# GpSimd issues most loads of a decode kernel, one packet per DMA engine and load

## The chip, the cores and the metric

The kernel runs on one core of a Trainium2 chip. A core has five engines, each with its own instruction stream: TensorE (PE: matrix products), VectorE (DVE), ScalarE (ACT), GpSimd (POOL) and SyncE (SP, which only issues transfers and waits). Sixteen DMA engines carry data from HBM into the core's on-chip memory; a transfer is issued by an instruction on one of the engines' streams, and ends by raising a semaphore by 16, one for each DMA engine. Other engines wait for semaphores to reach a value.

The metric is the device time of one execution in microseconds (us), as the median of the runs.

## What is computed

One new token attends to a cache, and a gated MLP of the same token is mixed in:

```python
g = sigmoid((x * gate_w).sum(-1, keepdims=True))          # one number
q = (x @ wq)                                              # 512 -> 32 heads x 128
scores = einsum("bhqd,bhkd->bhqk", q, k_cache) * Dh**-0.5 # 32 heads, 65536 cached rows
p = softmax(scores);  o = einsum("bhqk,bhkd->bhqd", p, v_cache)
a = o.reshape(1, 1, 4096) @ wo
b = (silu(x @ w_gate) * (x @ w_up)) @ w_down              # 512 -> 1792 -> 512
out = g * a + (1 - g) * b
```

All data are bf16. K and V have 32 heads x 65536 rows x 128, so 16.8 MB per head and cache and 1074 MB in all; wq and wo have 4.2 MB each, the three MLP weights 1.8 MB each. Each cached number is used once.

## The kernel before

One on-chip buffer, `ring`, holds four "places" of 8.39 MB, 64 KB per partition: K_A and K_B for the first and second half of a head's keys, V_A and V_B for its values. The places of a pair overlap: K_B begins at the middle of K_A, and V_B a quarter into V_A, so a load into one may start when the shared rows of the other have been used. `kv_dram[kind][h, u]` is half `u` of head `h`, laid out so that each of 128 partitions takes 256 consecutive rows, 64 KB in one piece. Weights use bytes that are free at the time (WQ among the V places at the start; WO, WG, WU and WD among the K places at the end).

For each head VectorE turns K in 32 pieces of 16 rows per partition (`turn`, L314, a blockwise transpose into four small buffers `kt`; semaphore `ktd` counts the pieces). TensorE multiplies each piece by the query (`scores`, L401, into the PSUM bank `psS`). When all 32 are done, VectorE takes the maximum per partition (L338, `s_mx`), GpSimd the maximum over partitions (L216, `s_ar`), ScalarE the exponentials with their sums (L251, `s_exp`), GpSimd the total of the sums (L218, `s_L`), and VectorE turns the probabilities (L340, `s_pb`). Then TensorE multiplies V: the rows of V_A in two parts (`flow`, L417; `va1` after rows 64 to 255), and, after the first half of the next head's scores, those of V_B (`vbd` when finished).

The order of the loads is written out by hand on SP's stream (L143 to L197), each load behind the wait that says its place is free. Per head `r` there are four: `K_A` of the next head when the first half of `K_B` has been turned (`ktd`), V_B when `va1` says that the rows of V_A it covers are done, `K_B` of the next head when the upper half of the new `K_A` has been turned (`ktd`), and V_A of the next head when V_B is done (`vbd`). `head(r, late)` holds this order; a loop runs it 30 times and once more with the two loads of `wo` added. At the start the q weights are issued first (L136), then K's first places in halves: upper half of K_A, its lower half (`s_k0a`), upper half of K_B (`s_k0b`), lower half of K_B. VectorE begins with the upper half of K_A (`A_ORDER`). At the end the last V_B place is cut into parts (`PARTS`, with the semaphores `MARKS`), and w_down into four, so that little work is left after the last landing. ScalarE issues only the two small inputs and the result.

GpSimd clears a few tiles, makes four copies of pieces of an identity matrix, and then does the two reductions over partitions per head, each behind its wait (L214 to L218).

Of the kernel before, what the change touches and what calls it, by code (L numbers as in the profile page):

```python
# [6 lines left out]
KB = 1024  # L7
CH = 16
NB = 4
K_A, K_B = 0, 32 * KB  # L10
V_A, V_B = 96 * KB, 112 * KB
# [6 lines left out]
ET = mybir.EngineType  # L18
# [8 lines left out]
def bass_gated_mix__mha_block_cached__swiglu_ffn__decode_kernel(  # L27
# [11 lines left out]
    out: bass.AP,  # L39
):  # L40
    _, H, S, Dh = A_k_cache.shape
    D = A_wq.shape[0]
    F = B_w_gate.shape[1]
    Dc = D // P
    FC = F // P
    ROWS = S // (2 * P)
    NCH = ROWS // CH
    SCALE = float(Dh) ** -0.5
    assert Dh == 128 and D == 512 and F % P == 0 and ROWS == 256 and H == 32
    L = H - 1  # L50
    A_ORDER = list(range(NCH // 2, NCH)) + list(range(NCH // 2))
    B_ORDER = list(range(NCH))
    PER = 2 * NCH

    with ExitStack() as ctx:
# [6 lines left out]
        def sem(name):  # L62
            return ctx.enter_context(nc.semaphore(name))
# [47 lines left out]
        sm = {n: sem(n) for n in names.split()}  # L111
# [4 lines left out]
        kv_dram = {"k": A_k_cache[0].rearrange("h (u p r) d -> h u p (r d)", u=2, p=P),  # L116
                   "v": A_v_cache[0].rearrange("h (u p r) d -> h u p (r d)", u=2, p=P)}

        def at(byte, n):
            return ring[:, byte // 2:byte // 2 + n]  # L120

        WQ, WO, WG, WU, WD = 144 * KB, 0, 0, 14 * KB, 64 * KB
        PARTS = ((192, 256), (0, 64), (64, 128), (128, 168), (168, 184), (184, 192))
        FLOW = 3
        MARKS = ("s_vb", "s_p2", "s_p3", "s_p4", "s_p5", "s_p6")
        WD_CUT = FC - 3
# [15 lines left out]
        @block.sync  # L142
        def _(sp):  # L143
            def load(dst, src, s):
                sp.dma_start(dst, src).then_inc(sm[s], 16)  # L145

            def place(kind, h, u, s):
                byte = {"k": (K_A, K_B), "v": (V_A, V_B)}[kind][u]
                src = kv_dram[kind][:, u]
                if isinstance(h, int):  # L150
                    src = src[h]
                else:
                    src = src[bass.ds(h, 1)].rearrange("h p n -> (h p) n")
                load(at(byte, ROWS * Dh), src, s)

            k0 = kv_dram["k"][0, 0]
            k1 = kv_dram["k"][0, 1]
            half = ROWS * Dh // 2
            load(at(K_A + 2 * half, half), k0[:, half:2 * half], "s_ka")
            load(at(K_A, half), k0[:, 0:half], "s_k0a")  # L160
            load(at(K_B + 2 * half, half), k1[:, half:2 * half], "s_k0b")
            sp.wait_ge(sm["ktd"], NCH // 2)
            load(at(K_B, half), k1[:, 0:half], "s_kb")
            sp.wait_ge(sm["s_q"], 1)
            place("v", 0, 0, "s_va")

            def head(r, late):
                sp.wait_ge(sm["ktd"], r * PER + (PER - NCH // 2))
                place("k", r + 1, 0, "s_ka")
                sp.wait_ge(sm["va1"], r + 1)  # L170
                place("v", r, 1, "s_vb")
                if late:
                    wo_dram = A_wo.rearrange("(p j) n -> p (j n)", j=32)
                    for q in range(2):
                        sp.wait_ge(sm["ktd"], r * PER + (PER + 3 * NCH // 4 + q * NCH // 4))
                        load(at(WO + q * 16 * KB, 16 * D), wo_dram[:, q * 16 * D:(q + 1) * 16 * D], "s_wo")
                sp.wait_ge(sm["ktd"], r * PER + (PER + NCH // 2))
                place("k", r + 1, 1, "s_kb")
                sp.wait_ge(sm["vbd"], r + 2)
                place("v", r + 1, 0, "s_va")  # L180

            with nc.Fori(0, L - 1, engines=[ET.SP]) as i:
                head(i, False)
            head(L - 1, True)
            sp.wait_ge(sm["s_wod"], 1)
            load(at(WG, Dc * F), B_w_gate.rearrange("(p c) f -> p (c f)", c=Dc), "s_wg")
            load(at(WU, Dc * F), B_w_up.rearrange("(p c) f -> p (c f)", c=Dc), "s_wu")
            sp.wait_ge(sm["ktd"], PER * H)
            wd_dram = B_w_down.rearrange("(p c) n -> p (c n)", c=FC)
            load(at(WD, WD_CUT * D), wd_dram[:, 0:WD_CUT * D], "s_wd")  # L190
            last = kv_dram["v"][L, 1]
            for n, ((r0, r1), s) in enumerate(zip(PARTS, MARKS)):
                if n == 1:
                    sp.wait_ge(sm["va1"], H)
                load(at(V_B + r0 * 256, (r1 - r0) * Dh), last[:, r0 * Dh:r1 * Dh], s)
            for j, s in ((FC - 3, "s_wd1"), (FC - 2, "s_wd2"), (FC - 1, "s_wd3")):
                load(at(WD + 2 * j * D, D), wd_dram[:, j * D:(j + 1) * D], s)  # L197

        @block.gpsimd
        def _(pool):  # L200
            nc.gpsimd.memset(xTz[:], 0.0).then_inc(sm["s_qd"], 1)
            nc.gpsimd.memset(qd[:], 0.0).then_inc(sm["s_qd"], 1)
            for m, n in enumerate(MARKS[1:]):
                nc.gpsimd.memset(hbuf[:, m], 0.0).then_inc(sm[n], 16 * L)
            nc.gpsimd.memset(hot[:], 0.0).then_inc(sm["s_hot"], 1)
            pool.wait_ge(sm["s_id"], 1)
            pool.wait_ge(sm["s_hot"], 1)
            nc.gpsimd.tensor_copy(hot[:, 31:128:32], ident[:, P - 4:P])
            for je in range(4):
                off = 64 * (je // 2) + je % 2  # L210
                last = nc.gpsimd.tensor_copy(sel[:, je, :].rearrange("p (g d) -> p g d", g=4),
                                             ident[:, off:off + 63:2].unsqueeze(1).to_broadcast([P, 4, 32]))
            last.then_inc(sm["s_sel"], 1)
            for h in range(H):  # L214
                pool.wait_ge(sm["s_mx"], h + 1)
                nc.gpsimd.partition_all_reduce(amx, mxs, P, RMAX).then_inc(sm["s_ar"], 1)  # L216
                pool.wait_ge(sm["s_exp"], h + 2)
                nc.gpsimd.partition_all_reduce(Lt, rsum, P, RADD).then_inc(sm["s_L"], 1)  # L218

        @block.scalar  # L220
        def _(act):
# [342 lines left out]
```

## Time and profile before

| | before |
|---|---|
| median of 3 runs | 2513.63 us (2513.57 to 2513.91) |
| span of the profiled execution | 2512.5 us; the page gives no other time of it |
| read from HBM | 1087.64 MB, 433 GB/s over the span |
| busy: PE, DVE, ACT, POOL | 1510.1, 1249.7, 43.0, 25.9 us |
| large loads (144 packets each) | 144, all issued by SP |

The span runs from the program's first instruction to the end of its last; a run's time holds also what lies around it. PE's busy time is modelled and overlaps itself, so 60% says nothing about how near TensorE is to its best. A DMA's row has its issuing instruction's time only; how long the data took is told by the time from issue to landing, which includes the time it stood behind earlier loads. The slices divide the span into 40 pieces of 62.8 us; a digit 9 means nine tenths or more.

### The profile page before, as it was taken

What the parts mean: (1) busy time and instruction counts of PE and PEld (TensorE: products, weight loads), DVE (VectorE), ACT (ScalarE), POOL (GpSimd) and SP (SyncE); (2) the same over time, 40 slices, a digit from 0 to 9 for tenths busy, and PEclk for the clock granted to TensorE, in tenths of its full rate; (3) what the DMA queues carried; (4) which work ended last, traced back from release to release, by engine and by line L of the source; (5) the groups of instructions that cost most, each with busy time, mean ns of one, the idle gap of its engine ahead of it and who ended that gap; (6) DMA issues with size and microseconds to landing.
All of it is one profiled execution on the core that took longest, in us unless ns stands there. A gap on an engine that the chain in (4) does not pass through costs nothing.

```text
span 2512.5 us, 25250 instructions
## 1 busy us (share of the span) xinstructions
PE 1510.1 (60%) x10158; PEld 574.4 (23%) x10158; DVE 1249.7 (50%) x1213; ACT 43.0 (2%) x142; POOL 25.9 (1%) x81
## 2 busy tenths in 40 slices
PE   5565655755656556566465565565655655656568
PEld 1222221222222222222222221222221222222222
DVE  5464553644545536446455364464553644645534
ACT  0000000000000000000000000000000000000000
POOL 0000000000000000000000000000000000000000
PEclk9877877878778777778787787777877777778779
DMA  9999999999999999999999999999999999999999
GB/s 418 434 434 434 434 434 434 434 434 434 434 434 434 434 434 434 434 434 434 434 434 434 434 434 434 436 435 435 435 435 435 434 434 435 434 436 434 434 433 395
DMA packets 20749, 1087.73 MB, mean 433 GB/s; under 512 B 2308, under 2 KB 2695, under 8 KB 2951
## 3 DMA queue, kind: packets, MB, share of 16 engines
q1 hardware_dynamic: 20736, 1087.64, 100.0%
q8 instruction: 4, 0.07, 0.0%
q14 instruction: 3, 0.02, 0.0%
q10 hardware_dynamic: 6, 0.00, 0.0%
HBM read 1087.64 MB, written 0.00 MB: 433 GB/s over the span
## 4 chain that ended last, share of the span: by engine, by line
DMA 75%; DVE 15%; issue 7%; PE 2%; DVEq 0%; SPq 0%; ACT 0%; POOL 0%
DMA ring<-in_A_k_cache_dram 74%; DVE kt L314 15%; PE psS L401 2%; DMA ring<-in_A_v_cache_dram 1%; DVEq L311 0%; SPq L145 0%; PE psW L417 0%; DVE st L325 0%; PE psY L423 0%; ACT pa L251 0%; DVE pb L340 0%; DVE st L338 0%; DVEq L324 0%; DVE fin L359 0%; SPq L136 0%
## 5 line engine op out<-in xcount | busy, mean ns | idle before, releaser
L401 PE MATMUL psS<-kt,zq 128*128 128x512 bf16 x4096 | 1132.7, 426 | 851.7 <-DVE kt L314 833.2
L314 DVE STREAM_TRANSPOSE kt<-ring 128x1024 uint32<-128x1024 uint32 x1024 | 1163.1, 1206 | 936.4 <-DMA ring<-in_A_k_cache_dram 936.4
L401 PEld LDWEIGHTS psS<-kt,zq 128*128 128x128 bf16 x4096 | 386.8, 104 | 1583.9 <-DVE kt L314 1120.7
L417 PE MATMUL psW<-ring,pb 128*4 128x512 bf16 x3584 | 253.5, 444 | 103.5 <-DVE pb L340 102.4
L417 PEld LDWEIGHTS psW<-ring,pb 128*4 128x4 bf16 x3584 | 93.9, 97 | 261.3 <-issue 184.4
L327 DVE COPY brow<-psW 128x512 f32<-128x512 f32 x32 | 22.1, 691 | 120.3 <-PE psW L417 120.3
L408 PEld LDWEIGHTS psO<-pb,ring 128*128 128x128 bf16 x2048 | 56.8, 98 | 0.6 <-DMA ring<-in_A_v_cache_dram 0.6
L408 PE MATMUL psO<-pb,ring 128*128 128x1 bf16 x2048 | 56.5, 163 | 0.4 <-DMA ring<-in_A_v_cache_dram 0.2
L330 DVE TENSOR_SCALAR lt<-psO,st,sc 128x4 f32 x32 | 9.4, 294 | 89.1 <-PE psO L408 89.1
L452 PE MATMUL psO<-id,brow 128*128 128x1 f32 x256 | 33.7, 253 | 25.6 <-DVE brow L327 24.8
L340 DVE STREAM_TRANSPOSE pb<-pa 128x512 bf16<-128x512 bf16 x32 | 22.8, 711 | 48.7 <-ACT pa L251 48.7
L249 ACT ACTIVATE st<-st 128x1 f32<-128x1 f32 x32 | 6.5, 203 | 2353.9 <-POOL st L216 2353.9
L338 DVE TENSOR_REDUCE st<-psS 128x1 f32<-128x512 f32 x32 | 22.1, 692 | 37.4 <-PE psS L401 37.4
L452 PEld LDWEIGHTS psO<-id,brow 128*128 128x128 f32 x256 | 31.0, 191 | 41.7 <-DVE brow L327 40.4
L216 POOL PARTITION_ALL_REDUCE st<-st x32 | 11.2, 351 | 2416.5 <-DVE st L338 2416.5
L251 ACT ACTIVATE pa<-psS,st 128x512 bf16<-128x512 f32 x32 | 22.0, 687 | 1.0
L428 PE MATMUL psF<-ring,om 128*1 (+1 forms) x32 | 13.1, 410 | 2.7 <-DMA ring<-in_A_wo_dram 2.7
L512 PE MATMUL psY<-ring,hot 128*128 (+1 forms) x32 | 13.6, 424 | 0.0
L218 POOL PARTITION_ALL_REDUCE st<-st x32 | 12.3, 384 | 36.4 <-ACT pa L251 36.4
L256 ACT COPY zq<-qd 128x16 bf16 x31 | 7.7, 248 | 0.0
L251 ACT ACTIVATION_READ_ACCUMULATOR pa<-psS,st 128x1 f32 x32 | 6.2, 193 | 0.0
L428 PE MATMUL psF<-ring,kt 128*1 128x512 bf16 x11 | 4.0, 542 | 2.9 <-DVE kt L353 2.9
(87 smaller groups left out, 53.2 us busy)
## 6 DMA issues: line engine op xcount, KB each, us to landing
ring<-in_A_k_cache_dram SPq DMA_DIRECT2D x4, 4096.0 KB, 27.5
ring<-in_A_v_cache_dram SPq DMA_DIRECT2D x3, 2048.0 KB, 17.3
ring<-in_A_wq_dram SPq DMA_DIRECT2D x1, 4096.0 KB, 12.3
ring<-in_A_wo_dram SPq DMA_DIRECT2D x2, 2048.0 KB, 10.5
ring<-in_B_w_gate_dram SPq DMA_DIRECT2D x1, 1792.0 KB, 20.6
ring<-in_B_w_up_dram SPq DMA_DIRECT2D x1, 1792.0 KB, 24.4
ring<-in_B_w_down_dram SPq DMA_DIRECT2D x1, 1408.0 KB, 12.8
ring<-in_A_v_cache_dram SPq DMA_DIRECT2D x1, 1280.0 KB, 20.8
```

Source lines behind the costliest of these rows:

```text
L218: nc.gpsimd.partition_all_reduce(Lt, rsum, P, RADD).then_inc(sm["s_L"], 1)
L251: nc.scalar.activation(pa[:], psS[:], ACT.Exp, bias=nbias, scale=SCALE, accum_out=rsum).then_inc(sm["s_exp"], 1)
L314: nc.vector.transpose(o, src).then_inc(sm["ktd"], 1)
L327: nc.vector.tensor_copy(brow[:], psW[:]).then_inc(sm["s_flc"], 1)
L338: nc.vector.reduce_max(mxs, psS[:], AX_X).then_inc(sm["s_mx"], 1)
L340: nc.vector.transpose(pb[:], pa[:]).then_inc(sm["s_pb"], 1)
L401: last = nc.tensor.matmul(psS[:], zw[je][c], ktb[n % NB][:, je // 2, :, je % 2], start=first and je == 0, stop=stop and je == 3)
L408: last = nc.tensor.matmul(psO[:, 0:1], at(base + r * 256, Dh), pb[:, col:col + 1], start=first and n == 0, stop=stop and n == len(rows) - 1)
L417: last = nc.tensor.matmul(psW[g:g + 4, :], pb[:, col:col + 97:32], at(base + r * 256, 4 * Dh), start=first and n < 4, stop=stop and n >= l ...
L428: return nc.tensor.matmul(psF[0:1, :], lhs, rhs, start=first, stop=stop)
L452: nc.tensor.matmul(psO[:, 0:1], brow[:, e * Dh:(e + 1) * Dh], id4[:, e:e + 1], start=e == 0, stop=False)
L512: return nc.tensor.matmul(psY[:], hot[:, bass.ds(31 - j, P)], w, start=first, stop=stop)
```

## The change

SP keeps eleven loads: the q weights, the lower half of the first K_A, the upper half of the first K_B, the last five parts of the last V place and the last three rows of `w_down`. The other 133 move to GpSimd's stream and are issued there with `single_packet=True`, which asks that what one DMA engine carries of one load be one packet. Waits and sizes of the loads are the same, except for two: the first half of K_A now waits for the q weights to have landed (`s_wq`), and the first part of the last V place stands behind the wait for the last maximum (`s_mx`). GpSimd's two reductions per head (`top`, `total`) stand among the loads; what was a loop on SP is written out for all heads on GpSimd.

```diff
         @block.sync
         def _(sp):
             def load(dst, src, s):
                 sp.dma_start(dst, src).then_inc(sm[s], 16)
...
             half = ROWS * Dh // 2
-            load(at(K_A + 2 * half, half), k0[:, half:2 * half], "s_ka")
-            load(at(K_A, half), k0[:, 0:half], "s_k0a")
-            load(at(K_B + 2 * half, half), k1[:, half:2 * half], "s_k0b")
-            sp.wait_ge(sm["ktd"], NCH // 2)
-            load(at(K_B, half), k1[:, 0:half], "s_kb")
-            sp.wait_ge(sm["s_q"], 1)
-            place("v", 0, 0, "s_va")
-
-            def head(r, late):
...
+            load(at(K_A, half), kv_dram["k"][0, 0, :, 0:half], "s_k0a")
+            load(at(K_B + 2 * half, half), kv_dram["k"][0, 1, :, half:2 * half], "s_k0b")
+            last = kv_dram["v"][L, 1]
+            sp.wait_ge(sm["va1"], H)
+            for (r0, r1), s in zip(PARTS[1:], MARKS[1:]):
+                load(at(V_B + r0 * 256, (r1 - r0) * Dh), last[:, r0 * Dh:r1 * Dh], s)
...
         @block.gpsimd
         def _(pool):
...
+            def load(dst, src, s):
+                nc.gpsimd.dma_start(dst, src, single_packet=True).then_inc(sm[s], 16)
...
-            for h in range(H):
+            pool.wait_ge(sm["s_wq"], 16)
+            load(at(K_A + 2 * half, half), kv_dram["k"][0, 0, :, half:2 * half], "s_ka")
+            pool.wait_ge(sm["ktd"], NCH // 2)
+            load(at(K_B, half), kv_dram["k"][0, 1, :, 0:half], "s_kb")
+            pool.wait_ge(sm["s_q"], 1)
+            place("v", 0, 0, "s_va")
+
+            def top(h):
                 pool.wait_ge(sm["s_mx"], h + 1)
                 nc.gpsimd.partition_all_reduce(amx, mxs, P, RMAX).then_inc(sm["s_ar"], 1)
+
+            def total(h):
                 pool.wait_ge(sm["s_exp"], h + 2)
                 nc.gpsimd.partition_all_reduce(Lt, rsum, P, RADD).then_inc(sm["s_L"], 1)
...
```

Three places matter. On GpSimd, the start and the first head: before, the setup of the reductions (an ISA row without a tile) and the first two heads' reductions follow each other directly.

```order
L211 COPY sel<-ident 128x128 x4
L216 ISA
L216 ISA st<-st 128x1 [waits s_mx]
L218 ISA st<-st 128x1 [waits s_exp]
L216 ISA st<-st 128x1 [waits s_mx]
L218 ISA st<-st 128x1 [waits s_exp]
```

After, on the same engine, from the same copies to the end of the first head and the K place that opens the second:

```order
L179 COPY sel<-ident 128x128 x4
L167 DMA ring<-in_A_k_cache_dram 128x16384 [waits s_wq]
L167 DMA ring<-in_A_k_cache_dram 128x16384 [waits ktd]
L167 DMA ring<-in_A_v_cache_dram 128x32768 [waits s_q]
L167 DMA ring<-in_A_k_cache_dram 128x32768 [waits ktd]
L191 ISA
L191 ISA st<-st 128x1 [waits s_mx]
L195 ISA st<-st 128x1 [waits s_exp]
L167 DMA ring<-in_A_v_cache_dram 128x32768 [waits va1]
L167 DMA ring<-in_A_k_cache_dram 128x32768 [waits ktd]
L167 DMA ring<-in_A_v_cache_dram 128x32768 [waits vbd]
L167 DMA ring<-in_A_k_cache_dram 128x32768 [waits ktd]
```

Four loads per head now stand between the reductions, each with its wait, and the reductions' setup follows the fourth load. On SP, the start before:

```order
L136 DMA ring<-in_A_wq_dram 128x16384 [waits barrier_Pool_Activation_PE_DVE_SP_release]
L142 UNCONDITIONAL_BRANCH
L145 DMA ring<-in_A_k_cache_dram 128x16384 x3
L145 DMA ring<-in_A_k_cache_dram 128x16384 [waits ktd]
L145 DMA ring<-in_A_v_cache_dram 128x32768 [waits s_q]
```

All of SP's large loads after the change (the rows left out are smaller pieces of V and `w_down`):

```order
L136 DMA ring<-in_A_wq_dram 128x16384 [waits barrier_Pool_Activation_PE_DVE_SP_release]
L142 UNCONDITIONAL_BRANCH
L145 DMA ring<-in_A_k_cache_dram 128x16384 x2
L145 DMA ring<-in_A_v_cache_dram 128x8192 [waits va1]
L145 DMA ring<-in_A_v_cache_dram 128x8192
```

Of the three K halves that SP issued at once, two are left, and after them SP waits for the end. On GpSimd, the end after the change, from the last V place 0 on:

```order
L167 DMA ring<-in_A_v_cache_dram 128x32768 [waits vbd]
L167 DMA ring<-in_B_w_gate_dram 128x7168 [waits s_wod]
L167 DMA ring<-in_B_w_up_dram 128x7168
L167 DMA ring<-in_B_w_down_dram 128x5632 [waits ktd]
L191 ISA st<-st 128x1 [waits s_mx]
L167 DMA ring<-in_A_v_cache_dram 128x8192
L195 ISA st<-st 128x1 [waits s_exp]
```

The first part of the last V place (the row 128x8192) moved from directly behind `w_down` to behind the last maximum, ahead of the last total.

More of the change, by code (lines that the diff above doesn't have):

```diff
@@ L145, in load @@
                 sp.dma_start(dst, src).then_inc(sm[s], 16)
[L147 to L157, printed above, removed]
@@ L158, in _ @@
-            half = ROWS * Dh // 2
-            load(at(K_A + 2 * half, half), k0[:, half:2 * half], "s_ka")
-            load(at(K_A, half), k0[:, 0:half], "s_k0a")
-            load(at(K_B + 2 * half, half), k1[:, half:2 * half], "s_k0b")
-            sp.wait_ge(sm["ktd"], NCH // 2)
-            load(at(K_B, half), k1[:, 0:half], "s_kb")
-            sp.wait_ge(sm["s_q"], 1)
-            place("v", 0, 0, "s_va")
-            def head(r, late):
[L168 to L188, printed above, removed]
-            wd_dram = B_w_down.rearrange("(p c) n -> p (c n)", c=FC)
-            load(at(WD, WD_CUT * D), wd_dram[:, 0:WD_CUT * D], "s_wd")
@@ L191, in _ @@
[L191 to L195, printed above, removed]
+            half = ROWS * Dh // 2
+            load(at(K_A, half), kv_dram["k"][0, 0, :, 0:half], "s_k0a")
+            load(at(K_B + 2 * half, half), kv_dram["k"][0, 1, :, half:2 * half], "s_k0b")
+            last = kv_dram["v"][L, 1]
@@ L205, in _, with place @@
             nc.gpsimd.memset(hot[:], 0.0).then_inc(sm["s_hot"], 1)
+            def load(dst, src, s):
+                nc.gpsimd.dma_start(dst, src, single_packet=True).then_inc(sm[s], 16)
+            def place(kind, h, u, s):
+                byte = {"k": (K_A, K_B), "v": (V_A, V_B)}[kind][u]
+                load(at(byte, ROWS * Dh), kv_dram[kind][h, u], s)
+            half = ROWS * Dh // 2
             pool.wait_ge(sm["s_id"], 1)
@@ L213, in _ @@
             last.then_inc(sm["s_sel"], 1)
-            for h in range(H):
+            pool.wait_ge(sm["s_wq"], 16)
[5 more added lines that the diff above has]
+            def top(h):
                 pool.wait_ge(sm["s_mx"], h + 1)
                 nc.gpsimd.partition_all_reduce(amx, mxs, P, RMAX).then_inc(sm["s_ar"], 1)
+            def total(h):
                 pool.wait_ge(sm["s_exp"], h + 2)
                 nc.gpsimd.partition_all_reduce(Lt, rsum, P, RADD).then_inc(sm["s_L"], 1)
+            for r in range(L):
+                pool.wait_ge(sm["ktd"], r * PER + (PER - NCH // 2))
+                place("k", r + 1, 0, "s_ka")
+                top(r)
+                total(r)
+                pool.wait_ge(sm["va1"], r + 1)
+                place("v", r, 1, "s_vb")
+                if r == L - 1:
+                    wo_dram = A_wo.rearrange("(p j) n -> p (j n)", j=32)
+                    for q in range(2):
+                        pool.wait_ge(sm["ktd"], r * PER + (PER + 3 * NCH // 4 + q * NCH // 4))
+                        load(at(WO + q * 16 * KB, 16 * D), wo_dram[:, q * 16 * D:(q + 1) * 16 * D], "s_wo")
+                pool.wait_ge(sm["ktd"], r * PER + (PER + NCH // 2))
+                place("k", r + 1, 1, "s_kb")
+                pool.wait_ge(sm["vbd"], r + 2)
+                place("v", r + 1, 0, "s_va")
+            pool.wait_ge(sm["s_wod"], 1)
+            load(at(WG, Dc * F), B_w_gate.rearrange("(p c) f -> p (c f)", c=Dc), "s_wg")
+            load(at(WU, Dc * F), B_w_up.rearrange("(p c) f -> p (c f)", c=Dc), "s_wu")
+            pool.wait_ge(sm["ktd"], PER * H)
+            load(at(WD, WD_CUT * D), B_w_down.rearrange("(p c) n -> p (c n)", c=FC)[:, 0:WD_CUT * D], "s_wd")
+            top(L)
+            r0, r1 = PARTS[0]
+            load(at(V_B + r0 * 256, (r1 - r0) * Dh), kv_dram["v"][L, 1, :, r0 * Dh:r1 * Dh], MARKS[0])
+            total(L)
         @block.scalar
```

## The prediction

> **What bounds the kernel now.** I read the page's second and third part first (slices and DMA queues), then the share line of the chain that ended last, then the times from issue to landing, and last the two ends of the time axis.
>
> ```profile
> span 2512.5 us, 25250 instructions
> ...
> DMA  9999999999999999999999999999999999999999
> GB/s 418 434 434 434 434 434 434 434 434 434 434 434 434 434 434 434 434 434 434 434 434 434 434 434 434 436 435 435 435 435 435 434 434 435 434 436 434 434 433 395
> ...
> q1 hardware_dynamic: 20736, 1087.64, 100.0%
> ...
> DMA 75%; DVE 15%; issue 7%; PE 2%; DVEq 0%; SPq 0%; ACT 0%; POOL 0%
> ```
>
> All 40 slices have the DMA engines at nine tenths or more; only the first (418 GB/s) and the last (395) move less than 433. TensorE and VectorE are not what ends the time. So the kernel lasts as long as 1087.64 MB need at this rate, plus the two ends: against 434, the first slice loses 62.8 us x 16/434 = 2.3 us and the last 62.8 x 39/434 = 5.6 us. No tuning of waits can win much; only a higher rate or shorter ends can, and an empty DMA queue would cost its full length.
>
> Whether the queue ever runs empty is told by the listing of DMA issues, whose last number is the median time in us from issue to landing:
>
> ```profile
> ring<-in_A_v_cache_dram SPq DMA_DIRECT2D x63, 32.2
> ring<-in_A_k_cache_dram SPq DMA_DIRECT2D x62, 29.2
> ```
>
> The next fence has the packet counts of two stretches that I chose for their packet sizes: 509.00 to 2054.46 us, which holds 80 loads of 8.39 MB, and 2490.000 to 2499.725 us, where rows of 16 KB are loaded (parts of the last V place).
>
> ```profile
> DMA packets 11521, 671.10 MB, mean 434 GB/s; under 512 B 1280, under 2 KB 1280, under 8 KB 1280
> ...
> DMA packets 288, 4.19 MB, mean 431 GB/s; under 512 B 32, under 2 KB 32, under 8 KB 32
> ```
>
> From the first: a full load takes 1545.46/80 = 19.318 us, and it is 128 data packets of 65,536 bytes plus 16 tiny ones; per DMA engine 8 rows of 64 KB and one end mark. So of the 29.2 us of a K load 9.9 us are waiting behind earlier loads, and of the 32.2 us of a V load 12.9: the queue always holds at least that much work when a load is issued.
>
> From the second: 9.725 us carry 288/16 = 18 packets per engine, 16 of 16 KB and 2 marks. Four times the half of that, 4 x 4.8625 = 19.450 us, move as many bytes per engine as one full load, with 24 data packets and 3 marks more. The difference, 0.132 us over 27 packets, is 4.9 ns per packet. This is the whole room in the middle: 9 packets x 4.9 = 44 ns of each 19.318 us.
>
> **The change part by part.** *One packet per engine and load.* GpSimd now issues 133 of the 144 loads (20736 packets / 144 per load = 144): K 2 halves and 62 places, V 63 places, output weights 2, gate, up and down 3, first part of the last V place 1. Each had 8 data packets and a mark per engine. If the 8 become one and the mark stays by itself, 7 x 4.9 = 34.3 ns per load go, all of it on the path, since the engines never rest: 133 x 34.3 ns = 4.6 us. Ends of this term: 0, if each row keeps its cost inside the packet; 133 x 44 ns = 5.9 us, if all nine costs vanish. I take 4.6, because the rows show the cost attached to a packet whatever its length.
>
> [...]
>
> *GpSimd issues in place of SP, steady state.* One head in the timeline (start, duration, engine, line):
>
> ```profile
> 139.63 0.33 SPq L145 DMA_DIRECT2D ring<-in_A_k_cache_dram  x1
> 149.62 0.69 DVE L338 TENSOR_REDUCE st<-psS 128x1 f32<-128x512 f32 x1 [1.17 <-PE psS L401]
> 150.40 0.35 POOL L216 PARTITION_ALL_REDUCE st<-st  x1 [75.34 <-DVE st L338]
> ...
> 151.89 0.38 POOL L218 PARTITION_ALL_REDUCE st<-st  x1 [1.14 <-ACT pa L251]
> 152.78 3.63 PE L417 MATMUL psW<-ring,pb 128*4 128x512 bf16 x64 [3.19 <-DVE pb L340]
> 155.73 0.33 SPq L145 DMA_DIRECT2D ring<-in_A_v_cache_dram  x1
> ...
> 178.66 0.33 SPq L145 DMA_DIRECT2D ring<-in_A_k_cache_dram  x1
> ```
>
> POOL's new order (K place 0, maximum, total, V place 1, K place 1, V place 0) is the order of these times, so no wait on POOL stands in front of something that is due earlier: between the K issue and the maximum lie 10.4 us after SP's 0.33, between the total's end (152.27) and the V issue 3.5 us. How long a load occupies POOL, no row shows. Bounds: SP's 0.33 us below; above, the 1.4 us from SP's first issue to data (worked out below). I take 1.5 us of added delay until data, since nothing else is near. It costs nothing: 9.9 us of queued loads hide it. Without that cover it would cost 133 x 1.5 = 200 us. One more thing moves on POOL, the setup of its reductions (first and last start in the last columns):
>
> ```profile
> L216 POOL PARTITION_ALL_REDUCE st<-st x32: 350/351/352, 73.2 to 2478.9; - x32
> L216 POOLq MODIFY_POOL_CONFIG  x2: 14/14/14, 4.4 to 4.4; - x2
> ```
>
> ```profile
> 62.40 0.34 SPq L145 DMA_DIRECT2D ring<-in_A_k_cache_dram  x1
> ```
>
> It stood at 4.4 us and now follows the issue of the K place that was issued at 62.40, with 10.8 us until the first maximum: cost zero while it stays under that; above, each microsecond delays the first V issue, which has 12.9 in hand.
>
> *The start.*
>
> ```profile
> 0.73 0.39 SPq L136 DMA_DIRECT2D ring<-in_A_wq_dram  x1
> 1.17 32.64 SPq L145 DMA_DIRECT2D ring<-in_A_k_cache_dram  x4
> ...
> 13.15 1.90 PE L381 MATMUL psY<-ring,xTz 128*32 128x512 bf16 x16 [4.10 <-DMA ring<-in_A_wq_dram]
> ...
> 24.26 1.25 DVE L314 STREAM_TRANSPOSE kt<-ring 128x1024 uint32<-128x1024 uint32 x1 [14.43 <-DMA ring<-in_A_k_cache_dram]
> ...
> 33.86 0.44 SPq L145 DMA_DIRECT2D ring<-in_A_v_cache_dram  x1
> ```
>
> ```profile
> 0.00:5.00 5.00, 0.16 (x1) 0.10 (x1) 2.22 (x13) 1.28 (x1) 2.36 (x17) 1.00 0.71 249
> ```
>
> The last row (last number GB/s) gives 1.245 MB in the first 5 us; at 434 GB/s that is 2.87 us, so data flow from 2.1 us, 1.4 us after the first issue. The q weights and three K halves (16.8 MB, 38.6 us) keep the engines busy until about 40.7. Now the first half that VectorE needs is issued by POOL only after the q weights have landed (13.1), with data at about 14.6; SP's two other halves fill the time, so nothing idles. If POOL's packet runs whole, it ends after one foreign packet of 32 KB (1.2 us) and its own 9.7 us, at 25.5, some 2 us later than before; VectorE starts at 26.3 instead of 24.26, and K's next half, which waits for 8 transposes, is issued later by the same 2 us: SP's four K issues ended at 33.81, the last began at about 33.4, 9.1 us after the first transpose; now 35.4, with data ready at 36.9. The queue lasts to 40.7: 3.8 us in hand, cost zero.
>
> *The end.*
>
> ```profile
> 2477.02 0.33 SPq L145 DMA_DIRECT2D ring<-in_B_w_down_dram  x1
> 2477.39 10.65 SPq L145 DMA_DIRECT2D ring<-in_A_v_cache_dram  x6
> ...
> 2478.95 0.35 POOL L216 PARTITION_ALL_REDUCE st<-st  x1 [85.38 <-DVE st L338]
> ...
> 2480.43 0.38 POOL L218 PARTITION_ALL_REDUCE st<-st  x1 [1.14 <-ACT pa L251]
> ...
> 2490.07 0.55 ACT L264 ACTIVATE kt<-psY 128x448 f32<-128x448 f32 x1 [9.73 <-PE psY L488]
> ```
>
> ```profile
> ring<-in_B_w_down_dram SPq DMA_DIRECT2D x1, 1408.0 KB, 12.8
> ```
>
> The first V part now waits for the last maximum: issued at 2479.3 instead of 2477.4. The down weights ahead of it land at 2477.0 + 12.8 = 2489.8, so 10 us of work still lie before it: zero. The total behind it starts perhaps 0.4 us late; VectorE's next step after using it waits for ScalarE at 2490.07, 9 us on: zero. SP's last eight loads wait for what they waited for.
>
> Sum: 4.6 us less, nothing more. The span of 2512.5 becomes 2507.9. The median of the runs, 2513.63, lies 1.1 us above the profiled span; with the same 1.1 us: 2509.0.
>
> **The rivals.**
> *Nothing gained:* the 4.9 ns belong to each row, not to the packet. Against it: the marks, 4 bytes long, fit the same 4.9 ns. 2513.6, give or take 1.
>
> *Alternation at the start:* POOL's and SP's loads share each engine row by row. Then POOL's half lands at 14.6 + 19.3 = 33.9, 8 transposes end at 43.0, data follow at 44.5, and the engines idle from 40.7: 3.8 us. With the gain, 2512.8.
>
> [...]
>
> *One slow engine:* every load needs all 16, so the slowest sets the pace. If POOL's way of issuing burdens one of them by 0.5%, 0.5% of 2508 is 12.5 us: 2513.6 - 4.6 + 12.5 = 2521.5; it decides from 0.4%. Nothing in this trace shows such an engine: 434 GB/s holds over 1545 us. [...]
>
> **How the numbers follow.** Fewer packets 0.50 (2507.7 to 2510.5, the likeliest case's own range); nothing gained 0.10; alternation 0.08; gap 0.20; slow engine 0.12. The bound of 0.2%, about what a measurement of this kernel can tell from no change, is 5.0 us: 2508.6. Half of the first case's range lies on each side of 4.6 and the bound just beyond, so faster gets 0.25 of its 0.50, same the rest with the two middle cases, 0.43, slower 0.32. The range starts at 2513.6 - 5.9 = 2507.7 and ends at 2522, which leaves about half of the two slow cases, 0.16, outside.
>
> **What would show it.** Right: a full load in 19.28 to 19.29 us in place of 19.318 (435 GB/s in the middle slices), issue to landing still near 29 and 32 us, the first transpose near 26, the first V part issued near 2475 with the queue still busy. Wrong: slices under 434 in the middle, a DMA share under 1.00 there (a gap), one late landing per load (a slow engine), or VectorE starting near 34 (alternation).

## The result: 9.2 us slower

The changed kernel takes 2523.07 us (median of 5 runs, 2522.7 to 2523.66) against 2513.91 for the kernel before in the same comparison (5 runs, 2513.57 to 2514.29): ratio 1.0036, 95% interval 1.0024 to 1.0049. That is 9.2 us slower, where 4.6 us faster was forecast, and 1.1 us beyond the end of the range. The times of attention kernels below are medians too; one run of an experiment took 7253 us for a reason that nothing on record shows, and the ratio given there leaves it out.

The page of the changed kernel, its slices and DMA queues:

```profile
span 2521.8 us, 24758 instructions
...
GB/s 365 432 432 432 435 432 433 432 432 438 439 435 432 433 433 433 432 432 436 441 433 433 432 435 433 432 432 432 441 437 433 432 435 433 432 433 432 438 438 393
...
q0 software_dynamic: 19152, 1068.38, 97.8%
q1 hardware_dynamic: 1584, 19.27, 1.8%
```

The middle is as before; the loss stands in the first slice, 365 GB/s in place of 418: 63 us x 53/434 = 7.7 us. GpSimd's queue (q0) shows 19152 packets for 133 loads, 144 each, as SP's did: 128 rows and 16 marks. The stretch from 509.00 to 2054.46 us, chosen before because it holds 80 loads, holds 80 loads again, to the packet:

```profile
DMA packets 11521, 671.10 MB, mean 434 GB/s; under 512 B 1280, under 2 KB 1280, under 8 KB 1280
```

So a full load takes 19.318 us as before, whether GpSimd or SP issues it. The steady state hides GpSimd's issuing too (issue to landing, us):

```profile
ring<-in_A_v_cache_dram POOLq DMA_DIRECT2D x63, 32.0
ring<-in_A_k_cache_dram POOLq DMA_DIRECT2D x62, 29.1
```

29.1 and 32.0 us stand where 29.2 and 32.2 stood. The first 70 us of the timeline hold the rest:

```profile
13.29 0.69 POOL L167 DMA_DIRECT2D ring<-in_A_k_cache_dram  x1 [8.90 <-DMA ring<-in_A_wq_dram]
...
38.45 1.25 DVE L318 STREAM_TRANSPOSE kt<-ring 128x1024 uint32<-128x1024 uint32 x1 [28.31 <-DMA ring<-in_A_k_cache_dram]
...
47.95 0.54 POOL L167 DMA_DIRECT2D ring<-in_A_k_cache_dram  x1 [33.97 <-DVE kt L318]
```

The half that VectorE needs first is there at 38.45 us in place of 24.26. The next K half, which needs 8 transposes of it, is issued at 47.95 in place of some 33.4, and by then everything issued earlier has landed. Two stretches of the changed kernel (the last two numbers of a row are the DMA engines' busy share and GB/s):

```profile
42.80:49.20 6.40, 6.35 (x28) 2.44 (x27) 6.40 (x7) 0.00 (x0) 1.06 (x2) 0.97 0.02 5
10.00:60.00 50.00, 21.11 (x106) 7.52 (x108) 19.12 (x20) 3.35 (x8) 1.75 (x3) 0.76 0.87 369
```

For 6.4 us nothing moves. Over the 50 us from 10 to 60 the rate is 369 GB/s; the kernel before has 434 there:

```profile
10.00:60.00 50.00, 28.20 (x124) 10.14 (x125) 26.01 (x26) 3.35 (x8) 0.00 (x0) 0.90 1.01 434
```

The difference is 50 x 65/434 = 7.5 us. This view counts a packet whole where it starts, which can be off by up to 2.4 us (16 rows of 64 KB) at the edges of a window. If each packet in the trace's records is counted by the part that has been moved, the changed kernel is at 60 us 8.5 us behind the kernel before in bytes. How the lag runs on is seen in the same instruction of both kernels, the first transpose of a K place, in heads 1 and 31; before, then after:

```profile
130.31 2.37 DVE L314 STREAM_TRANSPOSE kt<-ring 128x1024 uint32<-128x1024 uint32 x2 [12.65 <-DMA ring<-in_A_k_cache_dram]
...
2410.31 1.25 DVE L314 STREAM_TRANSPOSE kt<-ring 128x1024 uint32<-128x1024 uint32 x1 [16.47 <-DMA ring<-in_A_k_cache_dram]
```

```profile
138.97 1.25 DVE L318 STREAM_TRANSPOSE kt<-ring 128x1024 uint32<-128x1024 uint32 x1 [12.63 <-DMA ring<-in_A_k_cache_dram]
...
2419.29 1.25 DVE L318 STREAM_TRANSPOSE kt<-ring 128x1024 uint32<-128x1024 uint32 x1 [16.45 <-DMA ring<-in_A_k_cache_dram]
```

8.66 us late after 139 us, 8.98 after 2419, 9.3 at the end of the span: 2280 us of loads issued by GpSimd add 0.3. (By bytes the lag is 8.5 us from 60 to 139 us and 9.0 from 500 us to 2480 us; what the half microsecond between 139 and 500 us is, no run shows.)

Why the half is so late, the single packets of one DMA engine tell, from the trace's packet records (start in us; S a row of SP's, P one of GpSimd's, s and p their end marks; each row lasts 1.21 us):

```
S 12.11  S 13.31  S 14.52  S 15.73  S 16.94
P 18.15  S 19.36  P 20.57  S 21.78  P 22.99  S 24.20  P 25.41  s 26.62
P 26.62  S 27.83  P 29.04  S 30.25  P 31.46  S 32.67  P 33.88  S 35.09  p 36.30
S 36.30  S 37.51  S 38.72  S 39.93  s 41.14
```

Two things are in it. GpSimd's first row begins at 18.15, 4.9 us after its issue (the first on any engine at 17.06). Then the two queues take turns, row by row, so that its 8 rows take 17 us (18.15 to 35.09) and not 9.7; the end mark waits for one more row of SP's.

### The profile page after: what moved, and what is told of

The parts are those of the page before. It is cut to its first block, busy times and chain, and to the rows that moved or that the text cites. A ratio compares the mean times of both kernels' runs of the same rounds, so it can differ in the third digit from the quotient of the medians.

```text
span 2521.8 us, 24758 instructions
## 1 busy us (share of the span) xinstructions
PE 1479.6 (59%) x10029; PEld 574.6 (23%) x10158; DVE 1249.6 (50%) x1213; ACT 43.0 (2%) x142; POOL 97.3 (4%) x214
## 3 DMA queue, kind: packets, MB, share of 16 engines
q0 software_dynamic: 19152, 1068.38, 97.8%
## 4 chain that ended last, share of the span: by engine, by line
DMA 73%; DVE 16%; issue 8%; PE 2%; DVEq 1%; ACT 0%; POOL 0%
DMA ring<-in_A_k_cache_dram 73%; DVE kt L318 15%; PE psS L405 1%; DVEq L315 0%; DMA ring<-in_A_wq_dram 0%; PE psW L421 0%; PE psF L432 0%; DVE st L329 0%; PE psY L492 0%; DVE kt L352 0%; PE psY L427 0%; PE psO L412 0%; PE psO L456 0%; ACT pa L255 0%; DVE pb L344 0%
## 5 line engine op out<-in xcount | busy, mean ns | idle before, releaser
L405 PE MATMUL psS<-kt,zq 128*128 128x512 bf16 x3968 | 1102.2, 423 | 892.3 <-DVE kt L318 869.4
L167 POOL DMA_DIRECT2D ring<-in_A_k_cache_dram x64 | 34.0, 531 | 1339.1 <-DVE kt L318 1330.2
L167 POOL DMA_DIRECT2D ring<-in_A_v_cache_dram x64 | 35.1, 548 | 632.0 <-PE psO L412 477.0
```

The source lines that it names most:

```text
L167: nc.gpsimd.dma_start(dst, src, single_packet=True).then_inc(sm[s], 16)
L405: last = nc.tensor.matmul(psS[:], zw[je][c], ktb[n % NB][:, je // 2, :, je % 2], start=first and je == 0, stop=stop and je == 3)
```

## The experiments

The theory from here on: the 9.2 us are the empty queue at the start, caused by the late first half; the half is late because the two queues shared each DMA engine row by row (17 us for 8 rows) and because GpSimd's first row came late on busy engines (4.9 us after its issue); asking for single packets changes nothing. The rivals: the packets do gain in the middle and the start lost more than it shows, or GpSimd's issuing costs something with every load.

**One part undone: the first half back on SP.** The kernel is the changed one, but SP issues the three K halves in the old order. GpSimd keeps its other 132 loads, and one more of 1 KB raises `s_ka` by the 16 for which VectorE waits there.

```diff
+            load(at(K_A + 2 * half, half), kv_dram["k"][0, 0, :, half:2 * half], "s_k0c")
             load(at(K_A, half), kv_dram["k"][0, 0, :, 0:half], "s_k0a")
...
-            pool.wait_ge(sm["s_wq"], 16)
-            load(at(K_A + 2 * half, half), kv_dram["k"][0, 0, :, half:2 * half], "s_ka")
+            load(fin[0:1, :], xr_dram, "s_ka")
...
+            dve.wait_ge(sm["s_k0c"], 16)
             with nc.Fori(0, H, engines=[ET.DVE]) as i:
```

> [...] Theory (the 9.2 us are an empty queue at the start, because GpSimd's half alternated row by row with SP's, and GpSimd's packets gain nothing later): 2514.0 us, within 0.6 of the kernel before, first transpose at 24.3. Rival 1 (the packets do save 4.6 us in the middle, and the start lost 13.8): 2509.4. Rival 2 (GpSimd's way of issuing costs something with every load): 2522 or more.

Measured: 2513.53 us, ratio to the kernel before 0.9999 (0.9990 to 1.0008). Its timeline:

```profile
24.52 1.25 DVE L318 STREAM_TRANSPOSE kt<-ring 128x1024 uint32<-128x1024 uint32 x1 [14.77 <-DMA ring<-in_A_k_cache_dram]
...
34.02 0.56 POOL L168 DMA_DIRECT2D ring<-in_A_k_cache_dram  x1 [29.01 <-DVE kt L318]
```

The whole loss is gone, with 132 large loads still issued by GpSimd. So it belongs to this one half, and issuing the rest from GpSimd, 1064 MB, neither costs nor gains anything that can be measured. Both rivals fall.

**The flag alone.** Twice the loads were issued without `single_packet`: in the changed kernel, and in the kernel of the first experiment.

```diff
-                nc.gpsimd.dma_start(dst, src, single_packet=True).then_inc(sm[s], 16)
+                nc.gpsimd.dma_start(dst, src).then_inc(sm[s], 16)
```

> Edit: GpSimd's loads without single_packet, all else as in the changed kernel. Theory (the flag changes neither the cost of a row nor the alternation at this row size): 2523.0 us, within 0.7 of the changed kernel, first transpose at 38.4, full load in 19.318 us. Rival (the flag saved its 4.6 us and hid a larger loss): 2527.6, full load longer by 0.03 us or more.

Measured: 2522.88 us, ratio to the kernel before 1.0036 (1.0023 to 1.0049), as with the flag; first transpose at 38.77, and 80 loads in the same stretch.

> Edit: the kernel with GpSimd's first half back on SP (e1), without single_packet. Theory (the flag does nothing to the rate): 2513.6 us, within 0.4 of e1. Rival (the flag makes up for something that GpSimd's issuing costs in the middle): 2515 or more.

Measured: 2513.88 us, ratio 0.9999 (0.9991 to 1.0008), against 0.9999 with the flag. The flag is worth nothing here, neither in the rate (434 GB/s from 509.00 to 2054.46 us with it and without) nor in the turns that the queues take (first transpose at 38.45 us with it, 38.77 without).

**Fewer rival rows.** SP's second half waits until GpSimd's has landed.

```diff
             load(at(K_A, half), kv_dram["k"][0, 0, :, 0:half], "s_k0a")
+            sp.wait_ge(sm["s_ka"], 16)
             load(at(K_B + 2 * half, half), kv_dram["k"][0, 1, :, half:2 * half], "s_k0b")
```

> Edit: SP's second half (upper half of the first K_B) waits until GpSimd's half has landed, so that 8 rows per DMA engine stand against it, not 16. Theory (alternation row by row of 1.21 us): SP has moved 5 of its 8 rows when GpSimd's first row starts at 18.15 us; 3 are left, so GpSimd's 8 rows take 11 x 1.21 = 13.3 us and end at 31.5, the first transpose is at 33.5 in place of 38.45; the queue is empty for about 2.7 us while SP's second half is issued, and no more before the next half; about 2517.6 us. Rival (GpSimd's first load is late by itself, whatever stands beside it): the first transpose stays at 38, SP's second half is issued after that, and the queue is empty for 10 us or more: 2525 or later.

Measured: 2518.93 us, ratio 1.0020 (1.0011 to 1.0030).

```profile
13.44 0.69 POOL L168 DMA_DIRECT2D ring<-in_A_k_cache_dram  x1 [9.05 <-DMA ring<-in_A_wq_dram]
34.00 0.33 SPq L145 DMA_DIRECT2D ring<-in_A_k_cache_dram  x1
34.11 1.25 DVE L319 STREAM_TRANSPOSE kt<-ring 128x1024 uint32<-128x1024 uint32 x1 [24.14 <-DMA ring<-in_A_k_cache_dram]
```

On one engine GpSimd's rows now run from 18.17 to 31.48, as the alternation with 3 rows gives. The total is 1.3 us over the expectation. The first transpose came at 34.1, not 33.5, and SP's late half left this engine empty for some 3.4 us, not 2.7; and the engines ran short once more before the next K half, issued only at 43.61, which the expectation had ruled out (by bytes the kernel is 4.0 us behind at 40 us and 4.9 at 60).

**Shorter rival rows.** SP's halves are issued as four loads with rows of 16 KB.

```diff
-            load(at(K_A, half), kv_dram["k"][0, 0, :, 0:half], "s_k0a")
-            load(at(K_B + 2 * half, half), kv_dram["k"][0, 1, :, half:2 * half], "s_k0b")
+            quarter = half // 2
+            for c in range(2):
+                load(at(K_A + 2 * c * quarter, quarter), kv_dram["k"][0, 0, :, c * quarter:(c + 1) * quarter], "s_k0a")
+            for c in range(2, 4):
+                load(at(K_B + 2 * c * quarter, quarter), kv_dram["k"][0, 1, :, c * quarter:(c + 1) * quarter], "s_k0b")
```

> Edit: the changed kernel with SP's two halves cut into four loads with rows of 16 KB in place of 32 KB; GpSimd's half keeps its rows of 32 KB. Theory (the queues alternate by rows, whatever their length): each of GpSimd's 8 rows waits for one row of 0.61 us in place of 1.21, and the rows of SP that are ahead of its first are half as long: first row near 16.3 us, last ends near 30.2, first transpose near 32, queue empty for about 2 us in place of 8: 2516.8 us. Rival (the engines share by bytes, or in packets of another size): first transpose at 38, 2523.0.

Measured: 2518.06 us, ratio 1.0016 (1.0007 to 1.0026); first transpose at 33.92. On one engine, one row of GpSimd's to one of SP's, though SP's are half as long:

```
P 17.85  S 19.05  P 19.66  S 20.87  P 21.48  S 22.69  P 23.29 ...
```

So rows took turns here, not bytes: GpSimd's start 1.81 to 1.82 us apart, one row of 1.21 us and one of 0.61. The total is 1.3 us over the expectation, and the first row did not come earlier, as it had been expected to: still 4.0 us and more after its issue at 13.07, though the rows ahead of it were shorter.

**No two queues at the start.** GpSimd issues all three halves, once behind the wait for the q weights, once without it.

```diff
-            load(at(K_A, half), kv_dram["k"][0, 0, :, 0:half], "s_k0a")
-            load(at(K_B + 2 * half, half), kv_dram["k"][0, 1, :, half:2 * half], "s_k0b")
...
             pool.wait_ge(sm["s_wq"], 16)
             load(at(K_A + 2 * half, half), kv_dram["k"][0, 0, :, half:2 * half], "s_ka")
+            load(at(K_A, half), kv_dram["k"][0, 0, :, 0:half], "s_k0a")
+            load(at(K_B + 2 * half, half), kv_dram["k"][0, 1, :, half:2 * half], "s_k0b")
```

> Edit: SP issues only the q weights at the start; GpSimd issues all three K halves after them, in the old order, behind the same wait for the q weights. No two queues have work at the same time at the start. Theory (alternation of two queues was the loss): the DMA engines are empty from 12.1 us until GpSimd's first data, 1.3 to 2.3 us after its issue at 13.3, that is for about 2.8 us; GpSimd's half then runs whole and the first transpose is near 26; no other gap; 2516.6 us. Rival (GpSimd's first load is late by itself, 3.8 us to its first data): 4.9 us empty, first transpose at 28, 2518.8.

Measured: 2517.08 us, ratio 1.0013 (1.0004 to 1.0022).

```profile
13.34 1.75 POOL L165 DMA_DIRECT2D ring<-in_A_k_cache_dram  x3 [8.96 <-DMA ring<-in_A_wq_dram]
27.31 1.25 DVE L318 STREAM_TRANSPOSE kt<-ring 128x1024 uint32<-128x1024 uint32 x1 [17.51 <-DMA ring<-in_A_k_cache_dram]
```

On empty engines its first row starts 1.4 us after the issue (14.74), on the last engine 2.2. So its first load is not late by itself; it is late beside SP's. The first transpose is still 3.1 us behind the 24.26 of the kernel before: the wait for the q weights has its own part in the lateness, and here it leaves the engines empty (from 12.71 to 14.74 nothing moves). The changed kernel without only that wait was not tried.

The second kernel leaves out `pool.wait_ge(sm["s_wq"], 16)` as well.

> Edit: as the one before, but GpSimd does not wait for the q weights and issues the three halves at about 4.4 us, in the order in which they are needed. Theory: the queue is never empty; the q weights share the engines with GpSimd's first rows and land some 3 us later, which nothing at this point waits for longer than the K half itself; 2514.0 us, within 0.7 of the kernel before. Rival (the later q weights hold up the first scores and with them the next K load past 41 us): 2516 or more.

Measured: 2513.64 us, ratio 1.0000 (0.9991 to 1.0009). The q weights land later (TensorE starts on them at 17.79 in place of 13.15), and nothing is lost by it. This is the change without its loss: GpSimd issues every K and V place up to the last, at the time of the kernel before.

**A late half without GpSimd.** The kernel before, with SP's K halves in another order.

```diff
-            load(at(K_A + 2 * half, half), k0[:, half:2 * half], "s_ka")
             load(at(K_A, half), k0[:, 0:half], "s_k0a")
             load(at(K_B + 2 * half, half), k1[:, half:2 * half], "s_k0b")
+            load(at(K_A + 2 * half, half), k0[:, half:2 * half], "s_ka")
```

> Edit: the kernel before, GpSimd issues nothing; only SP's order at the start is changed, with the half that VectorE needs first issued third of the three K halves. Theory (a late first half is enough, whoever issues it): it lands near 42.5 with the end of what is queued, the first transpose is at 43.5, the next K half is issued 9.4 us later at 52.9 and has data at 54.2; the queue is empty for about 12 us: 2526 us. Rival (the loss needs GpSimd's issuing): under 2516 us.

Measured: 2527.39 us, ratio 1.0053 (1.0037 to 1.0070), 1.4 us over the expectation.

```profile
43.62 1.25 DVE L314 STREAM_TRANSPOSE kt<-ring 128x1024 uint32<-128x1024 uint32 x1 [33.85 <-DMA ring<-in_A_k_cache_dram]
...
42.80:49.20 6.40, 3.87 (x10) 1.47 (x12) 5.58 (x6) 0.00 (x0) 0.00 (x0) 0.50 0.00 0
```

The lateness alone made a loss here, 13.5 us, without a second queue. The first 60 us account for the kernels together. The second column is the rate that the view shows; the third is how far a kernel is behind the kernel before in bytes moved, with each packet counted by the part that has been moved:

| kernel | GB/s from 10 to 60 us | us behind in bytes at 60 us | us over before (medians) |
|---|---|---|---|
| half third on SP | 319 | 13.0 | 13.5 |
| changed, no flag | 357 | 8.8 | 9.0 |
| changed | 369 | 8.5 | 9.2 |
| one rival half | 392 | 4.9 | 5.1 |
| shorter rival rows | 403 | 3.9 | 4.3 |
| halves on GpSimd | 408 | 3.2 | 3.3 |
| halves on GpSimd, early | 431 | -0.1 | -0.1 |
| half back on SP | 433 | -0.1 | -0.3 |

The largest part left over is 0.7 us, in the changed kernel; its twin without the flag has 0.2. One profiled execution stands here beside a median of several, and no run takes this rest apart.

**The price of a row and of a first row, by themselves.** Two kernels do nothing but load. The first:

```diff
+            for i in range(16):
+                eng.dma_start(ring[:, i * 2048:(i + 1) * 2048], k[h, 0, :, i * 2048:(i + 1) * 2048], **kw).then_inc(sm[s], 16)
```

with SP as `eng`, then GpSimd, then GpSimd with the flag; then three loads of SP beside one of GpSimd's, with the flag and without.

> No attention is computed and the result is zeros; only loads. Phase A: SP issues 16 loads with 128 rows of 4 KB; B: GpSimd the same without the flag; C: GpSimd with the flag; D: SP issues 3 loads with rows of 32 KB, and GpSimd beside them one of rows of 32 KB with the flag; E: the same without it. Theory (the cost belongs to each row): A, B and C all take 155.3 ns per row and engine, 20 us for 16 loads; in D and E GpSimd's 8 rows alternate with SP's one by one. Rival (the flag joins rows): C has 151 ns per row, and in D the 8 rows follow each other while in E they alternate. For the late first data (3.8 us from GpSimd's issue at the start of the changed kernel): if it is first use alone, D and E, late in the program, show 1.5 us; if it is SP's rows already taken up, they show 3.8 again.

Measured, 20 us within each of the three phases:

```profile
3.00:23.00 20.00, 0.00 (x0) 1.00 1.02 407
27.00:47.00 20.00, 5.73 (x12) 1.00 1.02 405
51.00:71.00 20.00, 5.74 (x12) 1.00 1.02 406
```

SP 407, GpSimd 405, GpSimd with the flag 406 GB/s: had the flag spared 7 of 8 row costs of 4.9 ns in rows that take 155 ns (rows of 4 KB start 155 ns apart in the kernel before), the last would be nearer 418. Beside SP's loads GpSimd's 8 rows alternate one by one, with the flag as without. And its first row, late in a program that had issued 32 loads from GpSimd, came 4.8 us after the issue in both: it is not a matter of first use.

The second, in four phases (A to D), put a later queue behind a busy one.

> No attention is computed and the result is zeros; only loads, in four phases with all landed between them. A: SP issues 2 loads with rows of 64 KB, GpSimd some us later one with rows of 32 KB. B: SP issues 24 loads with rows of 4 KB, GpSimd one of rows of 32 KB beside them. C: GpSimd issues 2 loads with rows of 64 KB, SP some us later one of rows of 32 KB. D: SP 4 loads with rows of 32 KB, GpSimd one beside them. What the first row of the later queue waits beyond 1.3 us from its issue: if a fixed time (first contact of a queue with a busy engine), 2.4 to 3.3 us in A, B and D alike; if a fixed count of rows, about 3 rows: 7 us in A, 0.5 us in B, 3.6 in D; if a fixed number of bytes (about 100 KB), 3.6 us in all. C tells whether SP's first row waits as long behind GpSimd's. In all phases rows alternate one by one once both queues have begun.

Measured, from issue to the first row on any engine: 4.6 us behind rows of 64 KB (A), 3.8 behind rows of 4 KB (B), 3.8 behind rows of 32 KB (D), and 4.5 for SP's first row behind GpSimd's of 64 KB (C). Against 1.2 us on empty engines (47.95 to 49.19 in the changed kernel). So it isn't a count of rows, and it isn't GpSimd. A fixed time of 2.6 to 3.4 us more and a fixed number of bytes (at 27 GB/s per engine, from 32 KB in 1.21 us, about 80 KB) both fit, and these runs do not part them: why the first row waits stays open.

## Why the prediction was wrong, by its own steps

*What bounds the kernel*: right. In these runs an empty queue cost its full length, and little else cost anything; every kernel of the table lies within 0.7 us of that account. ("Always holds" went further than its source: 29.2 and 32.2 us are medians.)

*One packet per engine and load, 4.6 us*: this step failed. The cost was read about rightly (single rows of 16 and 64 KB start 0.607 and 2.414 us apart in the kernel before, which gives 4.7 ns), but I let it belong to what the flag would join. In that trace every row was a packet, so nothing in it could tell a cost of the row from a cost of the packet. The lower end that I kept, 0, was the truth: 80 loads take 1545.46 us before and after, and without the flag nothing changes. For rows of 4 to 64 KB issued with this flag no run here shows a gain.

*GpSimd issues in place of SP, zero in the steady state*: right. Its issue takes 0.53 us (1.5 until data were assumed, 1.2 to 2.3 measured on empty engines), and the queue hides it: 29.1 and 32.0 us from issue to landing, 29.2 and 32.2 before. POOL's order held, and so did the setup of its reductions behind the second K place.

*The start, zero*: this step failed, and with it the sign. It rested on "if POOL's packet runs whole" and on data 1.5 us after the issue, a time read from engines that were empty. The packet did not exist as a unit (144 packets for each of the 133 loads), and on the busy engines the first row came 3.8 to 4.9 us after the issue. The first transpose stood at 38.45 where 26.3 was written, and the 3.8 us in hand became 6.4 us with nothing moving. A term put at zero measured 8.5 us by 60 us.

*The end, zero*: right; the last landing is 8.9 us late (2518.9 us for 2510.0), as the loads 2000 us earlier are.

*The rivals.* Alternation named the mechanism with its place and was right in it, but priced 3.8 us, because the same 1.5 us stood in its sum: it has the first data at 14.6, the half landed at 33.9 and the next data at 44.5, where 17.06 at the earliest, 38.45 (the first transpose) and 49.19 were measured. The next data came 4.7 us later than in that sum, and 3.8 becomes the 8.5 that were measured. It also carried the gain of 4.6 us along and so came out at 2512.8. "Nothing gained" was true as well. I had held these two apart with 0.10 and 0.08, though both follow from one cause, that a row and not a load was the unit here; together, with the first row at its measured time, they give the result. The gap and the slow engine, to which I gave 0.32, did not occur: 434 GB/s held from 179 to 2342 us, with the DMA engines' share at 1.00. The gap stood for a pause of each DMA engine between two of GpSimd's loads; that there is one, and its 0.1 us, were my guess, and no run shows either: 80 loads took 1545.46 us whoever issued them. The measured time came within 0.8 us of what I had put for it, 2522.3, by luck: its cause is another. Nor does a run show a slow engine: it would have stretched the 19.318 us of a load, which all 16 must finish.

## What to carry to other kernels

An urgent load should not share its time with loads that are not urgent, on whatever queue they are: put it ahead of them in the same queue (here 2513.53 us with the half ahead on SP, 2523.07 beside SP's halves, 2527.39 behind them). Holding the others back until it has landed is the weaker cure: in the one kernel that did so for one half, the engines stood empty for some 3.4 us until the held load began. Here a second queue did not add bandwidth (429 GB/s from 19 to 34 us in both kernels); it took half of the turns, row by row. And where one assumption stands behind two rivals, give them one chance together, and work out the time with both.

## What was not expected of the hardware

- Two queues with work for the same DMA engine took turns by rows: 32 KB against 32, 32 against 16, 64 against 32, 32 against 4. GpSimd's 8 rows against SP's 32 KB rows took 17 us, against 16 KB rows 14. The profile counts each of these rows as a packet of its own (144 per load, with the 16 marks).
- A queue's first row on any engine came 3.7 to 4.8 us after its issue when another queue kept the engines busy (3.7 with the half back on SP, 4.8 in the first kernel of loads alone), and 1.2 to 1.4 us when they were empty; for SP behind GpSimd as for GpSimd behind SP.
- Loads issued by GpSimd ran at the same pace as SP's to the nanosecond, 19.318 us for 8.39 MB, and 434 GB/s was held from 179 to 2342 us.
